# A gated linear recurrence followed by a SoLU feed-forward block: shorter weight conversion, first loads by batch, z turned from contiguous columns, and a new written sequence

## The chip, the cores and the metric

The kernel runs on one core of one Trainium2 chip. A core has five engines with a queue each, which run side by side and wait for one another through semaphores: TensorE (PE in the profile; PEld is its loading of weights), VectorE (DVE), ScalarE (ACT), GpSimd (POOL) and SyncE (SP), whose queue issues nearly all transfers here. The metric is the device time of one execution in microseconds. The kernel before took 447.55 us, the median of five runs (446.79 to 448.53).

## The reference

Inputs are q, k, v, a_re and a_im with 4 batches, 8 heads, 768 steps and 48 channels, all float32; the weights w_in (384 x 1024) and w_out (1024 x 384), which are given in float64, and g_ln (1024) in float32. The first block is a recurrence with a complex gate whose magnitude is held at 0.999 or below; only the real part is read out:

```python
scale = np.minimum(mag, 0.999) / (mag + 1e-06)
a_re_n, a_im_n = (a_re * scale, a_im * scale)
for t in range(S):
    new_re = ar * S_re - ai * S_im
    new_im = ar * S_im + ai * S_re
    kv = np.einsum('bhd,bhe->bhde', k[:, :, t], v[:, :, t])
    S_re, S_im = (new_re + kv, new_im)
    y[:, :, t] = np.einsum('bhd,bhde->bhe', q[:, :, t], S_re)
```

The heads of a step are put side by side (8 x 48 = 384 columns), which gives x with 3072 rows. The second block works row by row:

```python
h = x @ w_in
sm = softmax(h)                  # over the 1024 columns
solu = h * sm
ln = (solu - mean(solu)) / np.sqrt(var(solu) + 1e-06) * g_ln
out = ln @ w_out
```

## The kernel before, in words

The 768 steps are cut into 6 stretches of 128, and a stretch of one batch is a chunk; there are 24 chunks, numbered c = 4 * stretch + batch. Two chunks of one stretch form a group g; there are 12 groups. Within a chunk the recurrence becomes products: the running product of the gates is computed as the running sum of their logarithms and angles, q and k are multiplied by the grown and decayed factors and by cosine and sine, and then a masked product of scores, a product with v, and a carried state for each batch give the 128 rows of y.

The function `whole` does this. It defines each piece of work as a named step and then writes the steps out by hand in one sequence: the strings `START`, `EVEN`, `ODD` and `END`. The engines take their instructions in just this sequence, so it fixes the order in each queue. `START` runs once. Then a loop over n = 2 to 19 runs `EVEN` for even and `ODD` for odd n; in these, a number behind the colon is added to n, and g1, g2, g3 stand for group n // 2 plus 1, 2, 3. `END` runs once. SP's queue is in this sequence too: a transfer that has to wait holds up all transfers behind it.

The steps that the following speaks of:

- `load_ar`, `load_ai`, `load_q`, `load_k`, `load_v`, `load_vr` bring a group's inputs (L650, L660). ar and ai have 2 buffers, q, k and v have 3.
- `fetch:i`, `raised:i`, `convert:i` turn piece i of the weights from float64 to float32 with integer operations (L681; L688 and L690 on ACT; L696, L698 and L700 on DVE). There are 6 pieces of w_in with 512 columns and 8 of w_out with 384. The raw pieces have 6 buffers. `again` and `inspect` fetch and look at them a second time later. `mean`, `meansum` and `centre` (L714 to L724) fold g_ln and the mean over the 1024 rows into w_out.
- The gate chain of a group: `clamp`, `inverse` (ACT: Ln, Exp), `ratio`, `tangent`, `square`, `secant`, `size`, `eps`, `lnm`, then on PE `total` (tile f_L, L789), then `grow` and `decay` (ACT), `last` (a transfer of the last row), `ks` and `qs`; and with another table of functions on ACT (`trig`) `angle`, `on`, `phase` (PE, L843), `nearest`, `part`, `cos`, `sin`, and back with `exp`. In group 0 the first steps run in halves a and b, one for each chunk.
- `k2`, `q2` (L902) write k and q twice, times cosine and sine, into f_kq. For chunks 0 and 1, PE turns them (`kt`, `qt`) and ACT copies them (`kT`, `qT`). For the others `kqb` (L911) turns 32 x 32 blocks on DVE and `kqt0` (L916) moves the blocks with four DMAs into f_kqT.
- `score0`, `score1` (L958), `mask0` (L962), `values` (L990), `carry` (L998), `add` (L1007 to L1010) for the recurrence of a chunk.
- `turned_x` (L1024), `up0`, `up1` (L1030), `exp0` (L1035), `solu0` (L1039), `centred` (L1071), `spread` (L1074), `norm`, `down0`, `down1` (L1093), `scale` (L1097), `store` (L1102) for the feed-forward part. Between `solu0` and `down`, z must be turned. In chunks 0, 1, 2 and 23 (the list SHORT) PE does it (`zt`, `zT`); in the others `blocks` (L1058) turns 32 x 32 blocks on DVE and `away` (L1063) moves them with four DMAs into f_zT, from which `down` takes weights of 32 columns.

In `blocks`, column c * 128 + 4 * f + s of z goes to block s: the source is read with a step of four elements. So partition p of f_zT belongs to row c * 128 + p of w_out. PSUM holds h once (f_h), so `up` of the next chunk waits for `exp0` and `solu0` of the one before.

A second function, `general`, computes the same for any input and runs only if a check of the values at the end asks for it; the change doesn't touch it.

Of the kernel before, what the change touches and what calls it, by code (L numbers as in the profile page):

```python
# [11 lines left out]
FP = mybir.dt.float32  # L12
# [3 lines left out]
AF = mybir.ActivationFunctionType  # L16
# [3 lines left out]
P = 128  # L20
# [495 lines left out]
load_ar:0 load_ai:0 clampb:0 fetch:5 fetch:13 fetch:9 clampa:0 inverseb:0 ratiob:0 inversea:0 fetch:0 raised:5  # L516
tangentb:0 ratioa:0 squareb:0 raised:13 load_q:0 tangenta:0 secantb:0 sizeb:0 load_k:0 fetch:2 squarea:0
load_ar:1 fetch:11 raised:9 load_ai:1 secanta:0 convert:13 epsb:0 sizea:0 epsa:0 lnmb:0 lnma:0 fourthb:0
fourtha:0 total1:0 decay1:0 convert:5 convert:9 grow1:0 ks1:0 total0:0 grow0:0 decay0:0 trig:0 angleb:0 ks0:0
anglea:0 phase1:0 qs1:0 qs0:0 raised:0 phase0:0 nearest1:0 nearest0:0 raised:2 convert:0 part1:0 part0:0 cosb:0  # L520
load_vr:0 cosa:0 last:0 fetch:1 convert:2 sinb:0 clamp:1 sina:0 k2:0 q2:0 kt0:0 exp:0 qt0:0 inverse:1 load_v:0
k2:1 kT0:0 q2:1 qT0:0 ratio:1 raised:1 tangent:1 kt1:0 ends:0 convert:1 fetch:4 fetch:3 qt1:0 kT1:0 carry:1
fetch:6 raised:11 fetch:7 qT1:0 gain:0 turn_ends:0 kt0:1 tot:0 square:1 score0:0 convert:11 add:1 raised:4
score1:0 secant:1 kT0:1 onward:0 mask0:0 qt0:1 raised:3 fetch:12 fetch:8 raised:7 qT0:1 values:0 turned_x:0
kt1:1 fourth:1 qt1:1 kT1:1 up0:0 size:1 eps:1 convert:4 convert:3 qT1:1 up1:0 raised:12 convert:7 lnm:1 raised:6
raised:8 total1:1 convert:12 exp0:0 load_vr:1 total0:1 grow1:1 score0:1 decay1:1 convert:6 decay0:1 grow0:1
load_q:1 trig:1 load_k:1 convert:8 solu0:0 angle:1 carry:0 load_ar:2 fetch:10 score1:1 qs0:1 raised:10 phase1:1
phase0:1 nearest1:1 qs1:1 mask0:1 add:0 convert:10 nearest0:1 part1:1 mean:0 load_ai:2 part0:1 mean:2 ks0:1
clamp:2 mean:1 centred:0 mean:6 load_v:1 ks1:1 cos:1 mean:4 sin:1 last:1 k2:2 mean:3 mean:7 mean:5 values:1
zt0:0 meansum:0 load_k:2 load_vr:2 zt1:0 turned_x:1 q2:2 zT0:0 load_ai:3 centre:6 up0:1 exp:1 inverse:2 kqb:2  # L530
ratio:2 centre:5 kqt0:2 tangent:2 centre:0 centre:4 centre:3 up1:1 centre:2 spread:0 score0:2 centre:7 score1:2
exp0:1 square:2 secant:2 centre:1 size:2 mask0:2 eps:2 zT1:0 ends:1 down0:0 load_q:3 turn_ends:1 values:2 lnm:2
tot:1 total0:2 turned_x:2 total1:2 down1:0 load_q:2 fourth:2 k2:3 q2:3 decay1:2 grow0:2 decay0:2 solu0:1 norm:0
zt1:1 kqb:3 grow1:2 trig:2 up0:2 load_ar:3 angle:2 centred:1 zt0:1 scale:0 carry:2 qs1:2 again:1 last:2 ks1:2
onward:1 on:2 kqt0:3 zT1:1 phase0:2 store:0 zT0:1 phase1:2 spread:1 nearest1:2 score1:3 ks0:2 score0:3
nearest0:2 clamp:3 qs0:2 part1:2 part0:2 load_v:2 onward:2
"""
EVEN = """
add:0 cos:g1 mask0:1 up1:0 sin:g1 exp:g1 load_ai:g3 ends:g1 values:1 exp0:0 k2:2 q2:2 inverse:g2 norm:-1
down0:-1 kqb:2 solu0:0 ratio:g2 load_k:g2 down1:-1 turned_x:1 zt0:0 blocks:0 tangent:g2 zt1:0 again:-2 scale:-1  # L540
zT1:0 carry:1 k2:3 q2:3 inspect:-3 centred:0 spread:0 up0:1 kqt0:2 zT0:0 square:g2 secant:g2 size:g2 away:0
up1:1 kqb:3 eps:g2 lnm:g2 exp0:1 store:-2 score1:2 load_v:g2 add:1 score0:2 onward:g1 mask0:2 down0:0 solu0:1
total0:g2 store:-1 inspect:-2 total1:g2 fourth:g2 down1:0 norm:0 grow0:g2 decay0:g2 kqt0:3 blocks:1 turn_ends:g1
decay1:g2 grow1:g2 values:2 tot:g1 trig:g2
"""
ODD = """
angle:g2 scale:-1 qs0:g2 again:-2 turned_x:1 score1:2 on:g2 ks0:g2 load_ar:g3 score0:2 load_vr:g2 centred:0
ks1:g2 spread:0 phase0:g2 qs1:g2 phase1:g2 nearest0:g2 last:g2 nearest1:g2 clamp:g3 load_q:g3 away:0 part0:g2
part1:g2 carry:1 up0:1
"""  # L550
END = """
up1:20 mask0:21 cos:11 norm:19 store:18 sin:11 down0:19 exp:11 exp0:20 k2:22 q2:22 values:21 down1:19 kqb:22
solu0:20 k2:23 q2:23 turned_x:21 up0:21 centred:20 kqt0:22 score1:22 blocks:20 away:20 up1:21 spread:20 scale:19
kqb:23 score0:22 kqt0:23 down0:20 down1:20 mask0:22 norm:20 values:22 exp0:21 score0:23 solu0:21 blocks:21
score1:23 turned_x:22 up0:22 scale:20 mask0:23 store:20 away:21 up1:22 exp0:22 solu0:22 values:23 blocks:22
centred:22 turned_x:23 centred:21 down0:21 up0:23 spread:21 ends:11 spread:22 down1:21 norm:21 away:22 up1:23
norm:22 store:19 scale:21 down0:22 exp0:23 solu0:23 down1:22 zt0:23 scale:22 centred:23 store:21 zT0:23 zt1:23
spread:23 down0:23 zT1:23 norm:23 down1:23 scale:23 store:22 store:23
# [11 lines left out]
def whole(ctx, tc, flag, q, k, v, a_re, a_im, moe_w_in, moe_w_out, moe_g_ln, out):  # L570
# [40 lines left out]
    unit, quarter, small, mhalf, magic, mmagic = (bias[:, i:i + 1] for i in range(6))  # L611
# [32 lines left out]
    def load_steps(g):  # L644
        ti, b0 = g * GB // B, g * GB % B

        def load(nm, src, pl):
            def f():
                t = T[nm, g] = pl.tile([P, GB, DM], FP, tag=nm, name=f"f_{nm}")
                nc.sync.dma_start(out=t.rearrange("p b (h d) -> p (b h) d", d=D),  # L650
                                  in_=src[b0:b0 + GB, :, ti * P:(ti + 1) * P, :].rearrange("b h t d -> t (b h) d"))
            return f

        def reverse():

            vr = T["vr", g] = odds[g % 3]
            odd = v[b0:b0 + GB].rearrange("b h t d -> (b h) t d")[1::2]
            for r in range(0, P, 32):
                t0 = ti * P + P - 32 - r
                nc.sync.dma_start(out=vr[r:r + 32].rearrange("p b x w -> p (b x) w")[:, :, 16:],  # L660
                                  in_=odd[:, t0:t0 + 32, :].rearrange("h t d -> t h d"))

        return dict(load_ar=load("ar", a_re, ld), load_ai=load("ai", a_im, ld), load_q=load("q", q, ldv),
                    load_k=load("k", k, ldv), load_v=load("v", v, ldv), load_vr=reverse)

    def weight_steps():
# [11 lines left out]
        def fetch(i):  # L678
            w, wide, c, f0, n = pieces[i % len(pieces)]
            raw = rawp.tile([P, NW, 2], I32, tag="raw", name="f_raw")[:, 0:n]  # L680
            nc.sync.dma_start(out=raw.rearrange("p n u -> p (n u)"), in_=wide[:, c, 2 * f0:2 * (f0 + n)])  # L681
            T["raw", i] = raw

        def raised(i):
# [4 lines left out]
                                 scale=2.0 ** -29, bias=magic)  # L689
            nc.scalar.activation(out=y, in_=y.bitcast(FP), func=AF.Identity, bias=mmagic)  # L690

        def convert(i):
# [5 lines left out]
            nc.vector.scalar_tensor_tensor(out=x, in0=hi, scalar=-2 ** 30, in1=x, op0=OP.bitwise_and,  # L698
                                           op1=OP.bitwise_or)
            nc.vector.tensor_tensor(out=x, in0=x, in1=T["bits", i], op=OP.add)  # L700

# [317 lines left out]
    def ffn_steps(n):  # L1019
# [12 lines left out]

        def exp():
# [201 lines left out]
```

## Time and profile before

| | |
|---|---|
| median of 5 runs | 447.55 us (446.79 to 448.53) |
| the profiled execution, in all | 445.85 us |
| its span in the profile | 444.1 us |
| mean granted TensorE clock | 0.973 |
| HBM read and written | 38.87 and 4.72 MB |
| DMA issues into f_kqT | 88, 192 KB each, 3.4 us to landing (median) |
| DMA issues into f_zT | 80, 128 KB each, 2.9 us to landing (median) |
| table loads on ACT | 25 of 1283 ns |

Times in the profile are counted from the start of the span. The span leaves out a little on both sides of the program, so the profiled execution took 1.75 us more than it, and the median of the runs lies 1.70 us above that execution. A row of the page's groups gives the line, the engine, the operation, the tiles with their shapes, the count, then the busy time in us and the mean of one instruction in ns, and behind the second bar the time that the engine stood idle just before these instructions, and what ended most of it. Busy times of PE are modelled: its products overlap.

### The profile page before, as it was taken

What the parts mean: (1) busy time and instruction counts of PE and PEld (TensorE: products, weight loads), DVE (VectorE), ACT (ScalarE), POOL (GpSimd) and SP (SyncE); (2) the same over time, 40 slices, a digit from 0 to 9 for tenths busy, and PEclk for the clock granted to TensorE, in tenths of its full rate; (3) what the DMA queues carried; (4) which work ended last, traced back from release to release, by engine and by line L of the source; (5) the groups of instructions that cost most, each with busy time, mean ns of one, the idle gap of its engine ahead of it and who ended that gap; (6) DMA issues with size and microseconds to landing.
All of it is one profiled execution on the core that took longest, in us unless ns stands there. A gap on an engine that the chain in (4) does not pass through costs nothing.

```text
span 444.1 us, 13426 instructions
## 1 busy us (share of the span) xinstructions
PE 398.7 (90%) x5726; PEld 218.8 (49%) x5726; DVE 371.3 (84%) x516; ACT 282.7 (64%) x453; POOL 68.5 (15%) x141
## 2 busy tenths in 40 slices
PE   0238966989999999999999999999999999999992
PEld 0116643555755555645654554654655646545441
DVE  5689999878999999899999899899998998764310
ACT  3999996685776666656856756756757756620330
POOL 3000002103022041022121111120130130120210
PEclk9985898999999999999999999999999999999998
DMA  8984947486697797797798788878868666172210
GB/s 237 242 213 143 218 87 163 100 184 164 144 204 174 174 221 183 182 219 176 174 220 199 173 183 207 177 185 213 164 157 180 127 161 158 38 176 72 66 37 27
DMA packets 167716, 72.40 MB, mean 163 GB/s; under 512 B 142176, under 2 KB 155488, under 8 KB 167648
## 3 DMA queue, kind: packets, MB, share of 16 engines
q1 hardware_dynamic: 167504, 71.14, 69.6%
q8 instruction: 47, 0.77, 0.7%
q10 hardware_dynamic: 144, 0.33, 0.2%
q14 instruction: 21, 0.17, 0.1%
HBM read 38.87 MB, written 4.72 MB: 98 GB/s over the span
## 4 chain that ended last, share of the span: by engine, by line
PE 82%; DMA 5%; ACT 4%; DVE 4%; SPq 2%; issue 1%; POOL 0%; DVEq 0%; ACTq 0%
PE f_o L1093 29%; PE f_h L1030 26%; PE f_y L990 9%; PE f_score L958 6%; PE f_L L789 4%; PE f_phase L843 4%; PE f_d L998 3%; DMA f_kqT<-f_kb 2%; DMA f_raw<-in_moe_w_in_dram 2%; DVE f_kq L902 1%; DMA f_raw<-in_moe_w_out_dram 1%; SPq L916 1%; ACT f_bits L690 1%; ACT f_bits L688 1%; SPq L650 1%
## 5 line engine op out<-in xcount | busy, mean ns | idle before, releaser
L1093 PE MATMUL f_o<-f_w_out,f_zT 128*32 128x384 f32 (+1 forms) x1344 | 131.8, 487 | 0.2 <-ACT f_zT L1052 0.2
L1030 PE MATMUL f_h<-f_w_in,f_xT 128*128 128x512 f32 x288 | 130.4, 600 | 0.0
L1093 PEld LDWEIGHTS f_o<-f_w_out,f_zT 128*32 128x32 f32 (+1 forms) x1344 | 52.5, 114 | 64.6 <-issue 56.8
L1030 PEld LDWEIGHTS f_h<-f_w_in,f_xT 128*128 128x128 f32 x288 | 52.6, 190 | 59.4 <-issue 57.2
L911 DVE STREAM_TRANSPOSE f_kb<-f_kq 128x1536 f32<-128x1536 f32 x22 | 52.1, 2370 | 1.5 <-DMA f_kqT<-f_kb 1.2
L1071 POOL TENSOR_SCALAR f_less<-f_sum 128x1 f32<-128x1 f32 x24 | 13.1, 549 | 202.7 <-DVE f_z L1039 202.7
L1097 ACT ACTIVATE f_ot<-f_o,f_rs 128x384 f32<-128x384 f32 x24 | 13.8, 573 | 48.1 <-issue 36.6
L1058 DVE STREAM_TRANSPOSE f_zb<-f_z 128x1024 f32<-128x1024 f32 x20 | 43.4, 2170 | 0.1
L1039 DVE SCALAR_TENSOR_TENSOR f_z<-f_h,f_z 128x1024 f32<-128x1024 f32 x24 | 28.9, 1206 | 14.4 <-ACT f_z L1035 14.4
L1035 ACT ACTIVATE f_z<-f_h 128x1024 f32<-128x1024 f32 x24 | 24.4, 1017 | 24.5 <-PE f_h L1030 24.5
L958 PEld LDWEIGHTS f_score<-f_kqT 96*32 96x32 f32 x1536 | 31.7, 114 | 16.1 <-issue 8.4
L958 PE MATMUL f_score<-f_kqT 96*32 96x96 f32 (+3 forms) x1536 | 34.5, 242 | 5.2 <-DMA f_kqT<-f_kb 5.0
L990 PE MATMUL f_y<-f_att,f_v 128*16 128x128 f32 (+1 forms) x384 | 37.4, 280 | 0.6 <-DVE f_att L962 0.6
L990 PE MATMUL f_y<-f_att,f_vr 128*32 128x128 f32 x384 | 37.2, 281 | 0.0
L789 PE MATMUL f_L<-f_lr,f_mats 128*128 128x384 f32 x48 | 19.9, 539 | 18.2 <-DVE f_lr L784 18.2
L962 DVE TENSOR_TENSOR f_att<-f_score,f_mats 128x1024 f32<-128x1024 f32 x24 | 29.1, 1215 | 7.0 <-PE f_score L958 7.0
L990 PE MATMUL f_y<-f_kqT,f_state 96*32 96x128 f32 (+1 forms) x640 | 32.3, 272 | 0.0
L1074 ACT ACTIVATE f_z<-f_z,f_less 128x1024 f32<-128x1024 f32 x24 | 27.5, 1145 | 3.7 <-DVE f_zb L1058 2.6
L1080 POOL TENSOR_SCALAR f_s<-f_s,f_sum 128x1 f32<-128x1 f32 x24 | 15.1, 630 | 75.6 <-ACT f_z L1074 74.9
L793 ACT ACTIVATE f_ai<-f_L 128x384 f32<-128x384 f32 x24 | 12.0, 499 | 22.6 <-PE f_L L789 22.6
L1024 ACT COPY f_xT<-f_y 128x384 f32<-128x384 f32 x24 | 11.3, 473 | 23.6 <-PE f_y L990 23.6
L990 PEld LDWEIGHTS f_y<-f_att,f_v 128*16 128x16 f32 (+1 forms) x384 | 20.9, 105 | 10.0 <-issue 8.5
(102 smaller groups left out, 641.4 us busy)
## 6 DMA issues: line engine op xcount, KB each, us to landing
f_kqT<-f_kb SPq DMA_DIRECT2D x88, 192.0 KB, 3.4
f_zT<-f_zb SPq DMA_DIRECT2D x80, 128.0 KB, 2.9
f_raw<-in_moe_w_in_dram SPq DMA_DIRECT2D x12, 512.0 KB, 6.2
f_raw<-in_moe_w_out_dram SPq DMA_DIRECT2D x16, 384.0 KB, 5.3
f_ar<-in_a_re_dram SPq DMA_DIRECT2D x12, 384.0 KB, 5.5
f_ai<-in_a_im_dram SPq DMA_DIRECT2D x12, 384.0 KB, 4.1
f_q<-in_q_dram SPq DMA_DIRECT2D x12, 384.0 KB, 4.6
f_k<-in_k_dram SPq DMA_DIRECT2D x12, 384.0 KB, 5.1
```

Source lines behind the costliest of these rows:

```text
L789: nc.tensor.matmul(out=ps, lhsT=tri, rhs=st["lr"][:, i * DM:(i + 1) * DM], start=True, stop=True)
L843: nc.tensor.matmul(out=ps, lhsT=turns, rhs=st["x0"][:, i * DM:(i + 1) * DM], start=True, stop=True)
L911: nc.vector.transpose(out=t, in_=T["kq", c].rearrange("p n h (f j) -> p j (n h) f", j=3))
L958: nc.tensor.matmul(out=scores[r0:r0 + 32, x, r:], lhsT=QK[:, r // 32, x], rhs=QK[:, r // 32:, H + x], start=True, stop=True)
L962: nc.vector.tensor_tensor(out=st["att"].rearrange("p (i u) t -> p i u t", u=2), in0=scores.rearrange("p (i u) t -> p i u t", u=2), in1=mat ...
L990: nc.tensor.matmul(**product)
L1030: nc.tensor.matmul(out=st["h"][:, half * 512:(half + 1) * 512], lhsT=st["xT"][:, c * P:(c + 1) * P], rhs=w_in[:, c, half * 512:(half + 1) ...
L1035: nc.scalar.activation(out=st["z"], in_=st["h"], func=AF.Exp, accum_out=sums[:, n:n + 1])
L1039: nc.vector.scalar_tensor_tensor(out=st["z"], in0=st["h"], scalar=1.0, in1=st["z"], op0=OP.mult, op1=OP.mult, accum_out=st["sum"][:, 0:1])
L1058: nc.vector.transpose(out=st["zb"], in_=st["z"].rearrange("p (c f s) -> p s c f", s=4, f=32))
L1074: nc.scalar.activation(out=st["z"], in_=st["z"], func=AF.Square, bias=st["less"], accum_out=st["sum"][:, 1:2])
L1093: nc.tensor.matmul(out=st["o"][rows], lhsT=zT, rhs=w_out[:, c], start=(c == 0), stop=(c == KF - 1))
```

## The change

It has four parts.

1. `raised` has one ACT operation in place of two; `convert` has the same three DVE operations with other constants and the addition in the middle.
2. For group 0, `load_ar` and `load_ai` are split into two transfers each, one for each chunk: `load_ara`, `load_aia`, `load_arb`, `load_aib`.
3. `blocks` reads 32 neighbouring columns for a block. So that the result fits, w_out's rows are fetched in another sequence (partition 4 * f + s gets row c * 128 + 32 * s + f), g_ln is fetched by four DMAs in the same sequence, and in the four chunks that PE turns, `exp0` writes z in that sequence and `solu0` works in four parts. Their four sums are added by two more POOL operations in `centred`.
4. `START`, `EVEN`, `ODD` and `END` are new. Two more table loads on ACT (`trig:0`, `exp:30`) stand at the start.

The core of the diff; of the four strings the whole of the new `EVEN` and `ODD` and the parts of the new `START` that matter here:

```diff
 START = """
+trig:0 load_ara:0 load_aia:0 exp:30 load_arb:0 clampa:0 inversea:0 ratioa:0 tangenta:0 load_aib:0 squarea:0
+secanta:0 clampb:0 fetch:9 sizea:0 inverseb:0 epsa:0 ratiob:0 fetch:5 tangentb:0 lnma:0 fetch:4 raised:5
+squareb:0 fetch:0 raised:9 convert:5 secantb:0 fetch:2 fourtha:0 sizeb:0 fourthb:0 epsb:0 total0:0 convert:9
+raised:0 decay0:0 lnmb:0 fetch:13 total1:0 load_q:0 grow0:0 load_k:0 raised:4 raised:13 grow1:0 convert:0
+raised:2 decay1:0 trig:30 convert:4 convert:13 convert:2 angleb:0 anglea:0 last:0 phase1:0 fetch:11 load_ar:1
...
+part1:0 sina:0 qs1:0 convert:11 cosb:0 load_vr:0 fetch:7 k2:0 kt0:0 sinb:0 q2:0 clamp:1 exp:0 ends:0 kT0:0 qt0:0
+k2:1 turn_ends:0 qT0:0 kt1:0 tot:0 inverse:1 q2:1 qt1:0 kT1:0 qT1:0 qt0:1 fetch:8 carry:1 ratio:1 kt0:1 score0:0
+add:1 kT0:1 tangent:1 qT0:1 fetch:12 score1:0 mask0:0 raised:1 square:1 qt1:1 raised:3 convert:1 fetch:10 kt1:1
...
 EVEN = """
+score0:2 tangent:g2 k2:3 square:g2 q2:3 secant:g2 fourth:g2 size:g2 kqb:3 load_k:g2 down0:0 eps:g2 spread:0
+lnm:g2 add:1 score1:2 load_ar:g3 exp0:1 total0:g2 total1:g2 grow1:g2 down1:0 decay0:g2 mask0:2 decay1:g2
+grow0:g2 kqt0:3 solu0:1 trig:g2 load_ai:g3 ends:g1 turn_ends:g1 ks1:g2 values:2 score1:3 angle:g2 score0:3
+ks0:g2 onward:g1 blocks:1 again:-5 on:g2 qs1:g2 phase0:g2 turned_x:2 last:g2 norm:0 tot:g1 away:1 carry:2
+nearest0:g2 qs0:g2 phase1:g2 mask0:3 nearest1:g2 add:2 scale:0 load_v:g2 part0:g2 part1:g2 cos:g2 inspect:-4
+clamp:g3 up0:2
 ODD = """
+centred:0 again:-3 inspect:-6 sin:g2 values:2 load_q:g3 k2:3 q2:3 exp:g2 kqb:3 store:-2 up1:1 down0:0 inverse:g3
+exp0:1 store:-1 turned_x:2 carry:2 solu0:1 centred:1 down1:0 spread:0 blocks:1 ratio:g3 up0:2 up1:2 norm:0
+scale:0 kqt0:3 load_vr:g2 away:1
...
@@ fetch
-            nc.sync.dma_start(out=raw.rearrange("p n u -> p (n u)"), in_=wide[:, c, 2 * f0:2 * (f0 + n)])
+            rows = wide[:, c, 2 * f0:2 * (f0 + n)]
+            if w is w_out:
+                rows = rows.rearrange("(s f) x -> f s x", s=4)
+            nc.sync.dma_start(out=raw.rearrange("p n u -> p (n u)"), in_=rows)
@@ raised
             nc.scalar.activation(out=y.bitcast(FP), in_=T["raw", i][:, :, 0].bitcast(U32), func=AF.Identity,
-                                 scale=2.0 ** -29, bias=magic)
-            nc.scalar.activation(out=y, in_=y.bitcast(FP), func=AF.Identity, bias=mmagic)
+                                 scale=-2.0 ** -51, bias=mtwo)
@@ convert
-            nc.vector.scalar_tensor_tensor(out=x, in0=hi, scalar=-2 ** 30, in1=x, op0=OP.bitwise_and,
-                                           op1=OP.bitwise_or)
             nc.vector.tensor_tensor(out=x, in0=x, in1=T["bits", i], op=OP.add)
+            nc.vector.scalar_tensor_tensor(out=x, in0=hi, scalar=2 ** 30 - 1, in1=x, op0=OP.bitwise_or,
+                                           op1=OP.bitwise_and)
@@ exp
+            if n in SHORT:
+                z, h = z.rearrange("p (c f s) -> p c s f", s=4, f=32), h.rearrange("p (c s f) -> p c s f", s=4, f=32)
+            nc.scalar.activation(out=z, in_=h, func=AF.Exp, accum_out=sums[:, n:n + 1])
@@ solu
+            parts = [(st["h"], st["z"])]
+            if n in SHORT:
+                parts = [(st["h"].rearrange("p (c s f) -> p s c f", s=4, f=32)[:, s],
+                          st["z"].rearrange("p (c f s) -> p s c f", s=4, f=32)[:, s]) for s in range(4)]
+            for i, (h, z) in enumerate(parts):
+                nc.vector.scalar_tensor_tensor(out=z, in0=h, scalar=1.0, in1=z, op0=OP.mult, op1=OP.mult,
+                                               accum_out=st["sum"][:, 2 + i:3 + i])
@@ blocks
-            nc.vector.transpose(out=st["zb"], in_=st["z"].rearrange("p (c f s) -> p s c f", s=4, f=32))
+            nc.vector.transpose(out=st["zb"], in_=st["z"].rearrange("p (c s f) -> p s c f", s=4, f=32))
@@ centred
+            if n in SHORT:
+                half, total = st["sum"][:, 2:4], st["sum"][:, 0:1]
+                nc.gpsimd.tensor_tensor(out=half, in0=half, in1=st["sum"][:, 4:6], op=OP.add)
+                nc.gpsimd.tensor_tensor(out=total, in0=st["sum"][:, 2:3], in1=st["sum"][:, 3:4], op=OP.add)
@@ gain
+        for s in range(4):
+            nc.sync.dma_start(out=g_ln[s:P:4], in_=moe_g_ln.rearrange("(c s f) -> f s c", s=4, f=32)[:, s])
```

## The prediction

> **What bounds the kernel now.** I read the page first (engine shares, the 40 slices), then the busy times in three stretches, then the chain that ended last, then the groups by shape, and last the queue of each engine in order of time.
>
> ```profile
> span 444.1 us, 13426 instructions
> PE 398.7 (90%) x5726; PEld 218.8 (49%) x5726; DVE 371.3 (84%) x516; ACT 282.7 (64%) x453; POOL 68.5 (15%) x141
> PEclk9985898999999999999999999999999999999998
> ...
> 0.00:92.88 92.88, 55.79 (x570) 34.03 (x571) 76.86 (x143) 72.97 (x123) 9.52 (x24) 0.89 0.74 177
> 92.88:436.20 343.32, 342.85 (x5156) 184.76 (x5156) 294.12 (x373) 209.16 (x329) 58.95 (x117) 1.00 0.71 162
> 436.20:444.10 7.90, 0.08 (x2) 0.00 (x0) 0.29 (x2) 0.58 (x1) 0.00 (x0) 0.77 0.12 37
> ```
>
> The columns of the three stretches are PE, PEld, DVE, ACT, POOL, granted clock, DMA share, GB/s. TensorE (PE) is busy for 342.85 of 343.32 us in the middle stretch: there only its own work sets the time. Ahead of 92.88 us it idles 37 us, while VectorE (DVE) and ScalarE (ACT) are at 83% and 79%. So the change can gain ahead of 92.88 us, or by giving TensorE less to do.
>
> ```profile
> 66.68 2.25 DVE f_kb L911
> 70.98 4.02 DMA f_kqT<-f_kb
> ...
> 88.19 4.45 DMA f_kqT<-f_kb
> 92.88 1.28 PE f_score L958 x34
> ...
> 136.85 5.35 PE f_h L1030 x12
> 142.20 1.24 PE f_score L958 x34
> ...
> 152.30 1.10 PE f_score L958 x34
> ...
> 378.88 5.15 PE f_h L1030 x12
> ...
> 391.09 2.77 PE f_h L1030 x6
> 393.86 0.68 PE f_score L958 x17
> 394.54 2.79 PE f_h L1030 x6
> 397.34 0.68 PE f_score L958 x17
> ```
>
> The chain (start, length) says who hands over: DVE turns k and q of chunk 3 (`kqb:3`, 83.91 to 86.2 us), a transfer brings them, and the scores of chunk 3 start at 92.88, after which only TensorE is in the chain. The last rows show a price of order: `up` and `score` halved and alternated take 2.77+0.68+2.79+0.68 = 6.92 us, undivided 5.35+1.24 = 6.59. One more stretch of full 128x128 products (up, L, phase, turns) between products in 32-wide pieces costs 0.33: about 0.19 on entering (up is 5.15 behind phase, 5.35 else), 0.14 on leaving (scores 1.24 behind up, 1.10 else).
>
> ```profile
> L911 DVE STREAM_TRANSPOSE f_kb<-f_kq 128x1536 f32<-128x1536 f32 x22 | 52.1, 2370 | 1.5 <-DMA f_kqT<-f_kb 1.2
> L1058 DVE STREAM_TRANSPOSE f_zb<-f_z 128x1024 f32<-128x1024 f32 x20 | 43.4, 2170 | 0.1
> ```
>
> These are groups by shape (busy us, mean ns, idle before). The turn of z takes 2.12 ns an element with a source step of four elements, that of k and q 1.54 with three; a plain pass over 1024 elements (L1039) takes 1.21 us.
>
> [...] the 25 loads here have 1283. [...] here the granted clock is 0.54 at 30 to 40 us and 0.61 at 40 to 50.
>
> **The change part by part.**
>
> *One ScalarE operation a piece.* Removed: L690, 8 x 615 + 6 x 722 ns = 9.2 us of ACT, all ahead of 62 us. Some 3.3 us of it is in the chain (0.72+0.61+0.61+0.72+0.61). VectorE still does three operations a piece. Their reordering I cost at nothing, bounds -0.1 to +0.1 us a piece (before, a dependent successor starts 0.13 us after the end).
>
> *First loads by batch.* Four DMAs for two. The first ar landed for DVE at 5.46 us and ai at 7.20; with half the bytes I take 4.2 and 5.0. ACT has two more table loads at the start (2.57 us): 0.72 + 3 x 1.28 = 4.6 us, just before the first clamp is done (4.8), so they are hidden; if the load comes sooner, they cost up to 0.5. But six weight pieces now lie ahead of q and k in SP's queue, and `last:0`, which waits for the decays (about 21.9), stands ahead of the loads for group 1.
>
> *z from contiguous columns.* 20 turns; if the step was the whole cost, each falls from 2.17 to about 1.2 us (bounds 1.1 and 2.17): 1.9 us of DVE per loop pass. TensorE covers this: worth nothing on the path. In chunks 0, 1, 2 and 23 the exponential writes, and four DVE operations of 256 elements read and write, with a step of 16 bytes. One operation of 1.24 us becomes four: at least 4 x 0.36 = 1.45, at most, with the doubled element cost, 4 x 0.6 = 2.4. Two of these chunks lie ahead of `kqb:3`: +0.4 to +2.4 us. In chunk 23 they are covered by `down:22` (5.3 us on PE); the two small POOL additions (0.3 to 0.5 each) by `down` as well. w_out's rows come in another sequence, with the same 3 KB each; g_ln by four issues for one, +1.9 us of SP, needed only at `mean:0`.
>
> *The new sequence, start.* By hand, with the durations above: lnm of half a at 13, squares and convert:5 next, the second half's at 17.5, decays done 21.9 (before 22.1), tables 23.3, phases done 27 (half clock), part, cos, sin; first `k2:0` at 30.6 (before 31.62). Then the array at half clock sets the pace: copies of kT0, qT0, `inverse:1` (1.8) between, kT1, qT1 at 37.0, then on PE a turn (1.05), carry (1.5), a turn (1.05) and the scores (2.36): `mask0:0` at 42.6 (before 42.93). The gain at the first load is mostly given back there. From `mask0:0` to the end of `kqb:3` DVE took 43.3 us before (42.93 to 86.2) and was busy for 40.3 of them; after, the same instructions lie between these two (7 weight pieces, all 8 centres, both k and q turns), summing to 0.1 more, and the split solu, for which I take +0.9 (the lower half of its bounds: DVE waits 1.8 us for PE in this stretch, 0.67 at a mask and 1.12 at tot, and the longer solu takes up some of that). So `kqb:3` ends at 42.6 + 43.4 + 0.9 = 86.9. Issue and landing take 6.5 (before 86.2 to 92.88 = 6.7): scores of chunk 3 at 93.4.
>
> *The new sequence, from there.* Before: 343.4 us of PE remain (436.3 - 92.88). After: the second half of up:2 now comes first, -2.9. The loop pass before: 5.35+1.24+2.60+1.49+2.72+0.15+1.90+1.10+1.51+0.81+5.35+1.90+5.16+0.67 = 31.95 (the chain's period is 31.96). After, with phase split by carry, up by values, score by down: .68+2.58+.55+1.49+2.72+.15+1.90+1.10+.83+.81+.83+2.58+1.90+2.77+2.72+.67+2.58+5.37 = 32.23, one full stretch more. 9 passes: +2.5. Outside the loop some three more stretches and a tot: +1.1. Remaining 344.1. The tail (last product to the end: scale, store, flag) is unchanged: 7.8.
>
> Sum: 93.4 + 344.1 + 7.8 = 445.3 us span, against 444.1. The profiled execution had 445.85 in all (1.75 beside its span), and the median of the runs stands 1.70 above it: 445.3 + 3.45 = 448.8.
>
> **Rivals.**
>
> *The start gains more than the loop loses (faster).* Place: DVE between `k2:0` and `k2:2`. If PE's slow turns don't hold it (ACT has 9.2 us less in its queue), DVE needs from 30.6 on only its own 28.2 + 1.4 (dependencies in seven pieces) + 0.5 = `k2:2` at 60.7 against 64.3. Then kqb:3 ends at 83.8, and the span is 83.8+6.5+344.1+7.8 = 442.2, the median 445.6. It decides once `kqb:3` ends before 85.0; with turns at full clock a further 2 us go. For it: DVE idled 14 of the 86.2 us before `kqb:3` ended, 10.4 of them ahead of the first k2. Against: carry, tot and the mask need PE, whose granted clock was 0.50 from 31.6 to 42.9 us and 0.53 still at 46 to 48.
>
> *A late zT in every pass.* In the odd half SP issues kqT (2.6), then four vr loads, then zT (2.6). kqb ends 21.5 us into the pass, so zT is issued to 29.4 and lands 2.9 later, at 32.3; `down0` wants it at 32.9. But four vr took 5.57 us at 180 us, and one zT set 4.37. A wait of 0.4 to 1 us in nine passes gives 452 to 458.
>
> *The turn of z is not cheaper.* Then DVE has 1.9 us a pass more; it enters the even half 3.8 us ahead of PE rather than 5.7, and `score1`, turned in the same pass, has 0.9 us to spare rather than 2.8: still hidden, 449 to 451.
>
> *The loop was VectorE's.* DVE is busy 30.72 of 31.96 us a pass. Were it the bound, the cheaper turn would give 9 x 1.9 = 17 us, 431. Against: PE's pieces in the tail, where DVE is idle, are as long as in the loop (5.37, 5.18, 1.11); I give it almost nothing.
>
> **How the numbers follow.** My forecast, within 446.5 to 451: 0.40. Start gains: 0.35. zT late: 0.20. The rest 0.05. Under 0.2% (0.9 us), about what a measurement of this kernel can tell from no change, lies 0.13, nearly all from my case. Faster 0.37: the first rival and a little of my case; slower 0.50: the rest of my case, the late zT, the dear turn. Range 442 to 456: down to the first rival with a warm array, up through most of the second.
>
> **What would show it.** Right: L690's successor gone, 14 operations on ACT; first k2 near 30.6; `kqb:3` ending near 87; scores of chunk 3 near 93.4; a pass of 32.2 us, with PE idle under 1 us in all; the z turn near 1.2 us. Wrong: `kqb:3` before 85 (first rival), a PE wait for a transfer into f_zT or f_kqT in the loop (second), a z turn of 2.17 us, split solu pieces of 0.6 us. If PE's alternation costs nothing in the loop, the pass stays at 31.96 and 2.5 us come off.

## The result and the profile after

The changed kernel takes 445.63 us (median of 28 runs, 443.94 to 448.90), the kernel before beside it 447.55 (49 runs). The ratio is 0.9962, with a 95% interval of 0.9950 to 0.9974: faster by 0.38%, or 1.7 us. The forecast was 448.8, slower. The range (442 to 456) held the time; the sign was wrong.

The page of the kernel after, its span, engines and granted clock by slice:

```profile
span 442.2 us, 13453 instructions
PE 402.8 (91%) x5726; PEld 218.9 (50%) x5726; DVE 361.0 (82%) x540; ACT 280.4 (63%) x441; POOL 63.7 (14%) x149
PEclk9999988999999999999999999999999999999998
```

TensorE (PE) is busy 4.1 us longer than before (398.7), and yet the span is 1.9 us shorter: PE idles 39.4 us instead of 45.4. VectorE (DVE) has lost 10.3 us of work, which the span doesn't show.

The busy times of the kernel after, cut where the prediction cut them (columns as there: PE, PEld, DVE, ACT, POOL, granted clock, DMA share, GB/s):

```profile
0.00:91.14 91.14, 58.77 (x579) 33.14 (x583) 79.71 (x155) 70.55 (x114) 9.97 (x24) 0.96 0.75 175
91.14:435.38 344.24, 343.97 (x5152) 185.77 (x5151) 281.00 (x384) 209.24 (x327) 53.75 (x125) 1.00 0.71 163
435.38:442.20 6.82, 0.08 (x2) 0.00 (x0) 0.29 (x2) 0.58 (x1) 0.00 (x0) 0.71 0.13 43
```

The three terms of the sum are there one by one, in one execution of each kernel. The scores of chunk 3 start at 91.14 (before 92.88, forecast 93.4). From there PE has 344.24 us (before 343.32, forecast 344.1). What lies behind its last product takes 6.82 (before 7.90, forecast 7.8). So the start gave 1.74, the middle took 0.92, the end gave 1.08.

The chain that ended last, kernel after (start, length, what):

```profile
69.63 3.69 DVE f_w_out L734 x7
73.45 4.29 PE f_o L1116 x8
...
91.14 0.68 PE f_score L968 x17
...
150.07 0.87 PE f_phase L853 x2
150.94 0.81 PE f_d L1008 x48
151.75 0.84 PE f_phase L853 x2
```

Before, the chain went from `kqb:3` over a transfer to the scores at 92.88. Now it goes over the centring of w_out to `down0:0` at 73.45, and PE works without a gap from there; the scores of chunk 3 find their transfer landed (at 90.70, 0.4 us before they start). The rows at 150 show `carry` (f_d) between the two phases, which makes the additional stretch of full products that the prediction priced. `up` starts at 133.52, 165.81 and 198.10: a pass of 32.29 us (before 31.96, forecast 32.23).

The groups by shape, kernel after (busy us, mean ns, idle before):

```profile
L1076 DVE STREAM_TRANSPOSE f_zb<-f_z 128x1024 f32<-128x1024 f32 x20 | 24.8, 1242 | 0.4
L1058 DVE SCALAR_TENSOR_TENSOR f_z<-f_h,f_z 128x256 f32<-128x256 f32 x16 | 9.2, 639 | 9.7 <-ACT f_z L1049 9.7
```

The turn of z takes 1242 ns instead of 2170. With neighbouring columns it runs at 1.21 ns an element, the pace of a plain pass in this kernel (1219 ns for 1024 elements). The quarter solu takes 639 ns for 256 elements, 2.5 ns an element.

### The profile page after: what moved, and what is told of

Same layout as the page of the kernel before. It is cut to its first block, busy times and chain, and to the rows that moved or that the text cites. A ratio compares the mean times of both kernels' runs of the same rounds, so it can differ in the third digit from the quotient of the medians.

```text
span 442.2 us, 13453 instructions
## 1 busy us (share of the span) xinstructions
PE 402.8 (91%) x5726; PEld 218.9 (50%) x5726; DVE 361.0 (82%) x540; ACT 280.4 (63%) x441; POOL 63.7 (14%) x149
## 4 chain that ended last, share of the span: by engine, by line
PE 83%; DVE 8%; ACT 4%; issue 2%; DMA 1%; POOL 0%; DVEq 0%; POOLq 0%
PE f_o L1116 28%; PE f_h L1040 27%; PE f_y L1000 9%; PE f_score L968 6%; PE f_phase L853 5%; PE f_L L799 4%; PE f_d L1008 3%; DVE f_w_out L734 1%; DMA f_ar<-in_a_re_dram 1%; ACT f_bits L699 1%; DVE f_kq L912 1%; ACT L898 1%; DVE f_kb L921 1%; PE f_zt L1068 1%; PE f_turned L933 0%
## 5 line engine op out<-in xcount | busy, mean ns | idle before, releaser
L1116 PE MATMUL f_o<-f_w_out,f_zT 128*32 128x384 f32 (+1 forms) x1344 | 135.5, 489 | 0.5 <-DVE f_w_out L734 0.3
L1116 PEld LDWEIGHTS f_o<-f_w_out,f_zT 128*32 128x32 f32 (+1 forms) x1344 | 54.9, 114 | 65.8 <-issue 50.5
L1058 DVE SCALAR_TENSOR_TENSOR f_z<-f_h,f_z 128x1024 f32<-128x1024 f32 (+1 forms) x36 | 33.6, 961 | 22.9 <-ACT f_z L1049 22.9
L1049 ACT ACTIVATE f_z<-f_h 128x1024 f32<-128x1024 f32 x24 | 28.6, 1190 | 15.9 <-PE f_h L1040 15.9
L1000 PE MATMUL f_y<-f_att,f_v 128*32 128x128 f32 (+1 forms) x384 | 37.0, 275 | 0.4 <-DVE f_att L972 0.4
L968 PE MATMUL f_score<-f_kqT 96*32 96x32 f32 (+3 forms) x1536 | 35.3, 237 | 2.0 <-DMA f_kqT<-f_kb 2.0
L1094 POOL TENSOR_SCALAR f_less<-f_sum 128x1 f32<-128x1 f32 x24 | 5.1, 214 | 190.0 <-DVE f_z L1058 162.7
L856 ACT ACTIVATE f_f<-f_phase,f_bias 128x384 f32<-128x384 f32 x24 | 13.9, 581 | 27.1 <-PE f_phase L853 26.9
L853 PE MATMUL f_phase<-f_x,f_mats 128*128 128x384 f32 x48 | 22.9, 578 | 6.7 <-ACT f_x L839 6.7
L912 DVE TENSOR_TENSOR f_kq<-f_cs,f_k 128x768 f32<-128x768 f32 x24 | 22.8, 951 | 4.1 <-ACT f_cs L870 3.4
```

Of the source, the lines that this page charges most:

```text
L853: nc.tensor.matmul(out=ps, lhsT=turns, rhs=st["x0"][:, i * DM:(i + 1) * DM], start=True, stop=True)
L912: nc.vector.tensor_tensor(out=t, in0=T["cs", g][:, i * H:(i + 1) * H], in1=heads(T[nm, g][:, i]).unsqueeze(2).to_broadcast([P, H, 2, D]), ...
L968: nc.tensor.matmul(out=scores[r0:r0 + 32, x, r:], lhsT=QK[:, r // 32, x], rhs=QK[:, r // 32:, H + x], start=True, stop=True)
L1000: nc.tensor.matmul(**product)
L1049: nc.scalar.activation(out=z, in_=h, func=AF.Exp, accum_out=sums[:, n:n + 1])
L1058: nc.vector.scalar_tensor_tensor(out=z, in0=h, scalar=1.0, in1=z, op0=OP.mult, op1=OP.mult, accum_out=st["sum"][:, 2 + i:3 + i])
```

## The experiments

Each kernel was timed beside runs of the kernel before on the same chip, so two of them are compared by their ratios; 0.001 of the ratio is 0.45 us. Medians in us.

| kernel | what it is | median | ratio to before, 95% interval |
|---|---|---|---|
| after | the change | 445.63 | 0.9962 (0.9950 to 0.9974) |
| two_ops | after, two ScalarE operations a piece | 452.29 | 1.0105 (1.0078 to 1.0132) |
| whole_loads | after, first loads whole | 446.97 | 0.9992 (0.9974 to 1.0010) |
| strided_z | after, z as before | 445.01 | 0.9947 (0.9932 to 0.9961) |
| b_one_op | before, one ScalarE operation a piece | 445.12 | 0.9948 (0.9928 to 0.9968) |
| b_one_op_loads | the same, first loads by batch | 445.67 | 0.9957 (0.9938 to 0.9977) |
| old_order | all of the change but the sequence | 448.23 | 1.0014 (1.0000 to 1.0029) |
| m1_carry | after, carry ahead of the phases | 442.89 | 0.9896 (0.9874 to 0.9918) |
| m2_up | and up whole | 442.04 | 0.9879 (0.9855 to 0.9902) |
| b_one_op_carry | b_one_op, carry ahead of the phases | 443.77 | 0.9914 (0.9883 to 0.9946) |
| warm | after, six more products on PE | 445.46 | 0.9952 (0.9936 to 0.9969) |
| warm3 | after, three more | 444.09 | 0.9925 (0.9898 to 0.9953) |
| short23 | after, chunks 0 to 2 turned on VectorE | 454.50 | 1.0144 (1.0115 to 1.0174) |
| best | m2_up + short23 + warm3 | 452.52 | 1.0100 (1.0070 to 1.0130) |
| m1_warm3 | m1_carry + warm3 | 442.15 | 0.9891 (0.9862 to 0.9920) |
| m2_warm3 | m2_up + warm3 | 440.73 | 0.9860 (0.9832 to 0.9888) |

### Which part made the start faster

**Two operations again.**

```diff
-                                 scale=-2.0 ** -51, bias=mtwo)
+                                 scale=2.0 ** -29, bias=magic)
+            nc.scalar.activation(out=y, in_=y.bitcast(FP), func=AF.Identity, bias=mmagic)
```

> The kernel after with the two ScalarE operations a weight piece put back (and VectorE's three in their old sequence); all else as after. Theory A (the start gains because ScalarE's queue is shorter): four pieces stand in the chain between 16 and 20.8 us, so each added operation of 0.61 to 0.72 us moves the first table load, the phases and the first k2 (29.25 us) by 2 to 2.6 us, and the median rises by 1.5 to 2.6 us, to 447.1 to 448.2. Rival B (the earlier first loads and the sequence make the gain, ScalarE's queue has room): first k2 moves by under 0.7 us, the median by under 0.5, to at most 446.1.

Measured: 452.29, 6.4 us above after by the ratios, more than twice what theory A asked. (VectorE's three operations went back to their old order with it.) ScalarE's (ACT) queue in time, two_ops, from the first half's L on:

```profile
18.22 0.72 ACT L701 ACTIVATE f_bits<-f_bits,f_bias 128x512 int32<-128x512 f32 x1
...
23.34 0.72 ACT L701 ACTIVATE f_bits<-f_bits,f_bias 128x512 int32<-128x512 f32 x1
23.97 0.47 ACT L807 ACTIVATE f_ar<-f_L 128x384 f32<-128x384 f32 x1
24.46 1.28 ACT L899 ACT_TABLE_LOAD   x1
```

The decays (L804, L807) stand behind the weight pieces in one queue; the table load that follows them starts at 24.46 instead of 20.84. That moves the first k2 from 29.25 to 32.97 and mask0:0 from 40.05 to 43.57. Between mask0:0 and mask0:1 a further 3.6 us come (66.23 for 59.06), where the pieces of 40 to 52 us stand in ACT's queue. So the new sequence doesn't merely gain from the removal, it can't do without it.

**First loads whole.**

```diff
-trig:0 load_ara:0 load_aia:0 exp:30 load_arb:0 clampa:0 inversea:0 ratioa:0 tangenta:0 load_aib:0 squarea:0
+trig:0 load_ar:0 load_ai:0 exp:30 clampa:0 inversea:0 ratioa:0 tangenta:0 squarea:0
```

> The kernel after with the first a_re and a_im loaded whole, as before (two DMAs for four); all else as after. Theory B (the earlier first loads make the gain): the first half's clamp starts at 5.5 instead of 4.5 us and its a_im comes at 7.2 instead of 5.4, so L of the first half comes 1.8 us later (15.0 for 13.2), the first k2 1 to 1.8 us later, and the median rises by 0.8 to 1.8, to 446.4 to 447.4. Rival A (ScalarE's queue): the first half has slack to the second, which sets the decays; first k2 moves by under 0.5, the median by under 0.4.

Measured: 446.97, by the ratios 1.3 us above after. The first k2 comes at 30.75 (+1.50), mask0:0 at 41.39 (+1.34), the k and q turn of chunk 3 at 83.69 (+1.53). A delay at the first load arrives at the end nearly whole: theory B holds too, beside A. Nothing of it was "given back".

**Everything but the sequence; and the operations alone in the old sequence.**

> The kernel after with the four written sequences of before (the first loads still by batch, each pair adjacent; no early table loads): everything in the change but the new sequence. If the operations alone make the start faster (one ScalarE operation, earlier loads), the start keeps most of the 1.7 us by which scores of chunk 3 came earlier, and the loop is back at 31.96 us a pass, so 442 to 444. If the new sequence makes the start, the start is as before or, with the split solu of chunks 0 to 2, later: 446.5 to 449.

> The kernel before with one ScalarE operation a weight piece, nothing else. Theory A (ScalarE's queue): in the chain of before three of the removed operations (0.72+0.61+0.61) stand ahead of the decays and two more later, so the first k2 comes 1.3 to 1.9 us earlier and the median falls by 1 to 3 us, to 444.5 to 446.5. Rival: the old sequence waits for the raw weight pieces (10.7 us in the chain) and for TensorE's slow turns, so the median falls by under 0.9 us, 446.7 to 447.5.

> The kernel before with one ScalarE operation a weight piece and the first a_re and a_im loaded by batch, the second batch's (whose clamp comes first in the old sequence) ahead. It parts the 3.1 us by which old_order (448.2) stands above b_one_op (445.1) into loads and z's layout. If z's layout costs them (split solu, strided exponential, g_ln by four issues): 444.1 to 445.3 here. If the loads by batch do (two more issues on SP's queue, transfers later behind them): 447 to 448.

Measured: 448.23, 445.12 and 445.67. In the old sequence one operation a piece gives 2.3 us (theory A's range). The earlier loads give nothing there: the first clamp starts at 4.74 instead of 5.52, but L, which the old sequence does for both halves together, stays at 15.98 (15.92) and the first k2 at 29.05 (28.99). With z's new layout as well, old_order stands 2.5 us higher (1.0014 against 0.9957); it also loads the halves of a_re ahead of those of a_im, another order than b_one_op_loads has, but its first k2 comes no later for that (28.50). Taking the parts in this order, the whole change is -2.3 (ScalarE) + 0.4 (loads, within the uncertainty of none) + 2.5 (z) - 2.3 (sequence).

The parts depend on each other. With z's old layout the new sequence gives only 0.4 us, within the uncertainty of none (strided_z, below, at 0.9947 against 0.9957 for b_one_op_loads, give or take 1.1 us). And one operation a piece alone (b_one_op, 0.9948) is as fast as the whole change (0.9962), within the uncertainty.

Where the 2.3 us come from in the old sequence, in the kernel before (start, length; f_L is `total`, L902 is `k2`, L962 is `mask0`):

```profile
11.49 0.72 ACT L690 ACTIVATE f_bits<-f_bits,f_bias 128x512 int32<-128x512 f32 x1
13.18 0.61 ACT L690 ACTIVATE f_bits<-f_bits,f_bias 128x384 int32<-128x384 f32 x1
15.27 0.61 ACT L690 ACTIVATE f_bits<-f_bits,f_bias 128x384 int32<-128x384 f32 x1
18.19 2.93 PE L789 MATMUL f_L<-f_lr,f_mats 128*128 128x384 f32 x4 [18.19 <-DVE f_lr L784]
31.62 0.96 DVE L902 TENSOR_TENSOR f_kq<-f_cs,f_k 128x768 f32<-128x768 f32 x1 [0.27 <-ACT f_cs L860]
42.93 1.21 DVE L962 TENSOR_TENSOR f_att<-f_score,f_mats 128x1024 f32<-128x1024 f32 x1
```

and in b_one_op:

```profile
15.92 2.92 PE L788 MATMUL f_L<-f_lr,f_mats 128*128 128x384 f32 x4 [15.92 <-DVE f_lr L783]
28.99 0.95 DVE L901 TENSOR_TENSOR f_kq<-f_cs,f_k 128x768 f32<-128x768 f32 x1
40.28 1.21 DVE L961 TENSOR_TENSOR f_att<-f_score,f_mats 128x1024 f32<-128x1024 f32 x1
```

Three of the removed operations stand among the steps of the first gate chain in ACT's queue, ahead of L. Without them L starts 2.27 us sooner, the first k2 2.63 and mask0:0 2.65. Between k2:0 and mask0:0 nothing is gained: 11.31 us in before, 11.29 in b_one_op, and the same to 0.03 us in the three other kernels with the old sequence. VectorE (DVE) is busy for 10.76 and 10.74 us of this stretch and shows no wait in it. So VectorE's own queue sets mask0:0 in the old sequence, and TensorE's pace doesn't: the 64 scores take 2.36 us in before and 1.33 in b_one_op, where they are done 3.3 us ahead of the mask.

**z as before.**

```diff
-            nc.vector.transpose(out=st["zb"], in_=st["z"].rearrange("p (c s f) -> p s c f", s=4, f=32))
+            nc.vector.transpose(out=st["zb"], in_=st["z"].rearrange("p (c f s) -> p s c f", s=4, f=32))
```

(with w_out's rows, g_ln, exponential, solu and sum of before)

> The kernel after with z laid out as before: the turn of z reads with a step of four elements (2.17 us for 1.24), w_out's rows and g_ln are loaded in their own sequence, and exponential and solu of chunks 0, 1, 2 and 23 are whole again. Theory (TensorE sets the loop, VectorE the start): the dearer turn costs nothing, and the start gains what the split solu (four of 0.64 and four accumulator reads for one of 1.22, in two chunks ahead of kqb:3) and the strided exponential cost, 2.5 to 3.2 us: 442.4 to 443.1. Rival (the new loop needs the cheaper turn): VectorE has 0.9 us more a chunk, TensorE waits in the loop, and the median is above 446.

Measured: 445.01, and by the ratios 0.7 us below after, the intervals overlapping. The dearer turn (18.6 us of DVE over 20 turns) costs nothing that shows, as theory said. The start's gain is half seen: the k and q turn of chunk 3 starts at 79.64 instead of 82.16, 2.5 us sooner, but `down0:0` only at 72.60 instead of 73.45. So in the new sequence the turn of chunk 3 is no longer alone in setting the end, and the 2.5 to 3.2 us of the theory didn't come. The rival isn't wholly excluded: in the one profiled execution the shortest pass takes 32.28 us, as in after, but the mean of seven is 32.73 (after 32.39), with halts of PE like those described further down.

### The slow array

> The kernel after with six further products (128x384, result not read) on TensorE between the first phases and the first turn of k, where it idles for 4.6 us: the array goes on working. If TensorE's slow turns and carry (1.96 us for eight turns, 1.50 for the first carry) still hold the start, they are done at full speed, mask0:0 starts 1 to 2 us sooner than 40.05, and the median falls by up to 1.6 us, to 444.0. If VectorE's own work sets the start, mask0:0 comes sooner but kqb:3 doesn't, and the median stays within 0.4 of 445.6.

> The kernel after with three further products (result not read) on TensorE between the first phases and the first turn of k, so that they end at about 30.2 us, when the first turn starts. With six, the first turn came 3 us late and mask0:0 0.5 us late, so that the fast array gave back 2.5 us. If the slow array holds the start, mask0:0 comes at 38 to 39 instead of 40.05 us and the median falls by 0.6 to 1.5, to 444.1 to 445.0. If VectorE's own work holds it, the median stays within 0.4 of 445.6.

```diff
+    def warm():
+        ps = ps_t.tile([P, DM], FP, tag="t", padded_shape=[P, 512], name="f_warm")
+        for i in range(3):
+            nc.tensor.matmul(out=ps, lhsT=ident, rhs=mats[:, 0:3].rearrange("p n t -> p (n t)"), start=True, stop=True)
...
-part1:0 sina:0 qs1:0
+part1:0 warm:0 sina:0 qs1:0
```

Measured: 445.46 with six, 444.09 with three. PE's queue in warm3:

```profile
30.92 1.09 PE L933 MATMUL f_turned<-f_mats,f_kq 128*96 128x128 f32 x8
...
35.40 0.88 PE L1008 MATMUL f_d<-f_v,f_kq 128*32 128x48 f32 x48
...
36.79 1.33 PE L968 MATMUL f_score<-f_kqT 96*32 96x128 f32 x64
```

Eight turns take 1.09 us (after 1.96), the first carry 0.88 (1.50). In after, VectorE waits for the carry and for the scores:

```profile
37.62 0.55 DVE L1020 TENSOR_TENSOR f_state<-f_d,f_tot 96x384 f32<-96x384 f32 x1 [1.19 <-PE f_d L1008]
...
40.05 1.22 DVE L972 TENSOR_TENSOR f_att<-f_score,f_mats 128x1024 f32<-128x1024 f32 x1 [0.41 <-PE f_score L968]
```

In warm3 it shows neither wait. mask0:0 starts at 38.41 instead of 40.05, `down0:0` at 71.71 instead of 73.45, and by the ratios the time falls by 1.7 us, give or take 1.3. With six, the first turn starts 3 us late, at 33.24, but mask0:0 only 0.5: eight turns take 1.04 us there, and 2.5 us came back. Why the turns behind the added products are faster isn't shown: the granted clock from 30 to 40 us is 1.00 in after as in warm3.

The gain isn't the same in each execution. The same three products stand in three later kernels: in m1_warm3, m2_warm3 and best the eight turns took 1.33, 1.63 and 1.70 us, and mask0:0 came at 38.43, 39.14 and 40.36. Nor is the pace without them a constant: the 64 scores took 2.36 us in before and 1.51 in after, but 1.33 in b_one_op and in m1_carry (below), which has the start of after; neither has an added product. So the slow array did hold the start of the new sequence, as the prediction said, by the 1.6 us of these two waits; in the old sequence it held nothing at mask0:0.

### The price of a stretch, and what takes it back

```diff
-ks0:g2 onward:g1 blocks:1 again:-5 on:g2 qs1:g2 phase0:g2 turned_x:2 last:g2 norm:0 tot:g1 away:1 carry:2
+ks0:g2 onward:g1 blocks:1 again:-5 on:g2 qs1:g2 turned_x:2 last:g2 norm:0 tot:g1 away:1 carry:2 phase0:g2
```

for m1_carry, and for m2_up also

```diff
-centred:0 again:-3 inspect:-6 sin:g2 values:2 load_q:g3 k2:3 q2:3 exp:g2 kqb:3 store:-2 up1:1 down0:0 inverse:g3
+centred:0 again:-3 inspect:-6 sin:g2 up1:1 values:2 load_q:g3 k2:3 q2:3 exp:g2 kqb:3 store:-2 down0:0 inverse:g3
```

> The kernel after with carry moved in the even half from between phase0 and phase1 to ahead of phase0, so that phase0, phase1 and the first half of up are one stretch of full 128x128 products: one stretch less a pass. If a stretch costs 0.33 us, as the prediction priced it, a pass falls from 32.29 to 31.96 us, and the median by 9 x 0.33 = 3.0 to 442.6. If TensorE's pieces are only recorded differently, or the new place makes carry wait for the copy of x, the median stays at 445.6 or rises.

> As the one before, and the second half of up moved ahead of values in the odd half, so that phase0, phase1 and both halves of up are one stretch: two stretches less a pass than after. At 0.33 us each a pass falls to 31.63 us and the median by 6 us, to 439.6. If the price isn't causal: 445.6. If values, 2.6 us later, makes the copy of x and the next up late, there is a new wait for f_xT and the median lies between 442.6 and 448.

> The kernel before with one ScalarE operation a weight piece, and carry moved in the odd half from between phase1 and up0 to ahead of phase0, so that phase and up are one stretch. If a stretch costs 0.33 us: a pass of 31.62 us, and the median 9 to 10 x 0.33 us below the 445.1 of the same kernel with the old place of carry: 442.0. If the price of a stretch isn't causal: 445.1.

Measured: by the ratios -3.0 us for one stretch (forecast -3.0), -3.7 for two (-6), and -1.5 for one in the old sequence (-3). The chain of m1_carry shows the merged stretch, in a pass of 31.94 us (265.60 to 297.54):

```profile
282.15 0.68 PE f_d L1008 x48
282.83 1.49 PE f_phase L853 x4
284.32 2.58 PE f_h L1040 x6
```

carry and the phases take 0.68 + 1.49 instead of 0.87 + 0.81 + 0.84, 0.35 less. The shortest passes carry the price throughout: 31.95 us in before and 31.60 in b_one_op_carry, 32.28 in after, 31.93 in m1_carry, 12.89 + 18.72 = 31.61 in m2_up. In the times it came in full only for the first stretch; m2_up's second one gave 0.7 us, and the 1.5 of b_one_op_carry has an uncertainty of 1.7. Where the rest went is seen in the passes: over seven passes of m2_up (122.51 to 346.97) the mean is 32.07, after's over seven (133.52 to 360.28) is 32.39, and over seven of b_one_op_carry it is 32.12 against 32.10 in b_one_op, each in one execution. PE's queue in m2_up, one such pass:

```profile
143.84 0.39 PE L968 MATMUL f_score<-f_kqT 96*32 96x128 f32 x6
144.00 0.49 PE L1116 MATMUL f_o<-f_w_out,f_zT 128*32 128x384 f32 x1
144.32 0.73 PE L968 MATMUL f_score<-f_kqT 96*32 96x32 f32 x26
```

`down` and the scores hang for some 0.4 us between two of their products; the profile shows no semaphore that is late. In m1_carry the same at 185.89, at the last scores ahead of carry:

```profile
185.89 0.22 PE L968 MATMUL f_score<-f_kqT 96*32 96x32 f32 x1 [0.66 <-issue]
```

"issue" means that the profile shows nothing that PE waited for. Most of these halts stand at the scores, where PE has 64 short products in 1.1 us (in b_one_op_carry two stand at carry), and they come in some passes of every kernel whose passes are given here (in before one pass takes 32.50 us for 31.96). That PE's instructions came late there, as the expectation of m2_warm3 has it, is my reading; no run shows it. Besides, TensorE, now earlier, waits 1.6 us at 109 us for the transfer of chunk 4's k and q in m1_carry and m2_up.

> The kernel after with carry ahead of the phases (-2.7 us measured alone) and the three further products (-1.5 measured alone). If start and loop add up: 441.4. If the earlier start only runs into the transfer of chunk 4's k and q (TensorE waited 1.6 us for it at 109 us in each of these), 442.9.

> As the one before with the second half of up ahead of values too (-3.6 us measured for both moves). If they add up: 440.5. If TensorE's waits for instructions at the scores take back what the cleaner order gives (clean passes took 31.6, their mean 32.1): 441.5 to 442.5.

Measured: 442.15 and 440.73. Start and loop add up for m2 (by the ratios 4.6 us below after, of 3.7 + 1.7), and hardly for m1 (3.2, of 3.0 + 1.7); the intervals are 2.6 us wide, so this part stays open. m2_warm3 is the fastest kernel of the study, 1.40% below before (0.9860, 0.9832 to 0.9888).

### The short chunks on VectorE

```diff
-    SHORT = [0, 1, 2, 23]
+    SHORT = [23]
-decay1:1 load_q:1 total0:1 grow1:1 grow0:1 convert:12 convert:6 decay0:1 score0:1 solu0:0 trig:1 angle:1
+decay1:1 load_q:1 total0:1 grow1:1 grow0:1 convert:12 convert:6 decay0:1 score0:1 solu0:0 blocks:0 away:0 trig:1 angle:1
```

(likewise for chunks 1 and 2)

> The kernel after with chunks 0, 1 and 2 treated like the chunks of the loop: whole exponential and solu, z turned on VectorE and sent by DMA (solu, then blocks, then away), no turn of z on TensorE; only chunk 23 keeps TensorE's. VectorE: 1.22 + 1.24 us a chunk for four pieces of 0.56 with 0.08 each = 2.5, no change; ScalarE loses 1.0 us an exponential and two copies a chunk; TensorE loses 3 x 0.87 us of turns. If the layout's price in these chunks is what keeps the new code from gaining more, the median falls by 1.5 to 3.5 us, to 442.1 to 444.1. Rival: zT by DMA lands too late for down in the start, TensorE waits there, and the median is 445.5 or more.

> The kernel after with three edits at once: carry ahead of the phases and the second half of up ahead of values, chunks 0 to 2 like those of the loop, and the three further products. If they add up: 445.6 - 3.6 (measured for the first two) - 1.5 to 3.5 - 0 to 1.5 = 437.0 to 440.5. If the loop then waits for instructions or transfers that TensorE used to give time for, it stays at 440.5 to 442.

Measured: 454.50 and 452.52; the rival's side, and by more than theory or rival reckoned. SP's waits in short23 from 40 to 130 us by cause (us in total, times, longest), one row:

```profile
SPq L1080 <- DVE f_zb L1075: 16.5, 3, 10.5
```

DVE's queue in short23:

```profile
94.07 0.95 DVE L756 TENSOR_SCALAR_CACHE_REDUCE f_ar<-f_ar 128x768 f32<-128x768 f32 x1 [6.07 <-DMA f_ar<-in_a_re_dram]
```

and PE's waits:

```profile
PE f_score L967 <- DMA f_kqT<-f_kb: 9.0, 2, 6.5
```

The transfers of `away` (L1080) wait in SP's queue for DVE's turn, once for 10.5 us (from 69.6 to 80.2), and every load behind them waits along: a_re of group 3 is issued at 87.6 instead of 77.6, and DVE stands 6.07 us for it. The transfer of chunk 3's k and q stands behind these loads too: their turn ends at 84.22, but it is issued at 89.84, and the scores wait 6.5 us for it, until 96.86 (after 91.14). `down` wasn't late, as the rival had it: PE shows no wait for a transfer into f_zT. By this trace the place of the transfer in the queue was the price, not its landing; no run puts it elsewhere.

## Why the prediction was wrong

**The step that failed: the hand-made timeline of the start**, "`mask0:0` at 42.6 (before 42.93)", with its reason, "the array at half clock sets the pace", and the conclusion, "The gain at the first load is mostly given back there". mask0:0 started at 40.05. Half of the 2.55 us lies ahead of k2:0 (29.25, forecast 30.6): L of the second half started at 17.52, as forecast (17.5), but the table load after the decays at 20.84, while I had the decays done at 21.9. The other half lies behind k2:0: 10.8 us to mask0:0 for the forecast 12.0, 0.85 of it in the 64 scores. (The terms of the timeline after 37.0 add up to 42.96, not to 42.6.)

The reason was misread from before. There the stretch from k2:0 to mask0:0 took 11.31 us because VectorE's own queue filled it; the slow array ran beside it and held nothing, as b_one_op shows. The new sequence takes work out of that stretch. Seven of the 14 weight pieces are converted on VectorE ahead of k2:0 (before five) and none between k2:0 and mask0:0 (before two). VectorE is busy there for 9.10 us (before 10.76), and ahead of k2:0 it idles 6.4 us (before 10.4). Only then does the array hold the stretch, by the 1.6 us of waits. This is read from the two traces; no run moves these pieces alone.

**From mask0:0 on the sum held.** To the end of `kqb:3` 44.44 us (forecast 44.3): VectorE had 2.0 us more work there than before (42.25 for 40.26), and 0.8 less idle time, so 1.2 of the 2.0 arrived, for a forecast of 1.0. From there to the scores 6.65 (6.5). In this second one chance helped: PE was itself busy until 91.14, and the transfer had landed. "kqb:3 decides" was right for before and no longer for after.

**The loop: right.** A pass of 32.29 (32.23), the rest of PE's work 344.24 (344.1); the price of 0.33 us a stretch is there in the shortest passes, and in the time of m1_carry.

**The end: 1 us too long, not seen.** From ACT's last eviction to the end of the span: 7.19 us in before, 6.20 in after, and 6.15 to 6.38 in the nine experiments on after with its turns of z on TensorE or its old z layout; 7.15 to 8.88 in the four with the old sequence, 9.18 and 8.77 in short23 and best. Each kernel was profiled in one execution: that nine lie within 0.23 us speaks for the program rather than the execution, but the five with the old ending differ by 1.7 among themselves. The cause is open; the prediction had "The tail ... is unchanged". It is 1.0 of the 3.1 us by which the span was missed (2.26 start, 0.98 end, -0.14 loop).

**ScalarE's operations:** 9.2 us removed, as forecast, and worth 2.3 us in the old sequence, 6.4 in the new. "Some 3.3 us of it is in the chain" was nearer than the timeline made of it. Of convert in its new order no cost is seen, but no run has it alone.

**First loads:** 4.52 and 5.43 us (forecast 4.2 and 5.0), worth 1.3 us (give or take 1.0) in the new sequence and nothing that shows in the old. The two table loads are hidden: the second ends at 4.58, and the first logarithm waits for DVE's clamp until 5.12.

**z's turn:** 1242 ns (forecast 1.2 us), and worth nothing on the path, as forecast (strided_z). **Split solu:** four of 0.64 us, which the prediction had named as a sign of being wrong; 2.17 and 2.33 us from start to end in chunks 0 and 1, inside the bounds of 1.45 to 2.4, but 0.9 and 1.1 more than one operation (1.22), where I took 0.9 for both together. **Not in the sum at all:** the strided exponential, 2.05 us for 1.00 (L1049 against L1035), and one on ACT in each of these chunks: the step of 16 bytes in its writes doubled the operation. The prediction had put a cost on this step for DVE alone. The layout as a whole shows a price of 2.5 us in the old sequence and 0.7, within the uncertainty, in the new; its parts weren't tried apart.

**The rivals.** The first came true: k2:2 at 61.60 (60.7), `kqb:3` ended at 84.5 (83.8, deciding below 85.0), span 442.2, median 445.63 (445.6). That the last two are met to the tenth is luck: `kqb:3` was 0.7 us later than the rival had it, and the end 1.0 shorter. Its mechanism came in part: from k2:0 to k2:2 VectorE needed 32.35 us, not the 30.1 of its own work, and k2:0 came 1.35 sooner. A late zT: PE shows no wait for f_zT by transfer in any pass of after; in short23 a zT did hold up SP's queue in the start, but the loads behind it came late, not `down`. The dearer turn: its turn didn't come, and strided_z, where it is as dear as before, took 445.0, though without the split solu. The loop wasn't VectorE's.

## What to carry to other kernels

An in-order queue is read by what stands behind each item, not by its busy share: ACT was 64% busy, and yet three operations of 0.6 to 0.7 us in its queue held the first gate chain, and with it everything behind it, by 2.3 us. Before a slow engine is put into a hand-made timeline, look whether anything waits for it. In before the engine behind the slow products had a full queue of its own, so their pace cost nothing; in after two pieces of work had left that queue, and the pace cost 1.6 us. In a reordering, count the switches between full and narrow products on PE. Each stretch costs 0.33 us a pass here, and taking one out of each pass was worth 3.0 us, more than the 1.7 of the whole change; the second gave only 0.7. And a part of a change can be as good as the whole: one ScalarE operation less, alone, was.

## What the runs showed of the hardware

- Three products without use, in PE's idle time, made the kernel 1.7 us faster (warm3, give or take 1.3). The eight turns behind them took 1.09 us there and 1.33 to 1.70 in three other kernels with the same products (after 1.96). The granted clock of the record doesn't tell it in time: after has 1.00 between 30 and 40 us, while its eight turns took 1.96 us there (1.08 later).
- An exponential that writes with a step of 16 bytes takes 2.05 us for 1024 columns, one that writes in sequence 1.00; a DVE product with such a step 639 ns for 256 columns, 1219 for 1024 without. A stream transpose with neighbouring columns takes 1242 ns, with a step of 16 bytes 2170.
- PE's halts, most of them at the scores, 0.2 to 1.4 us with nothing late that the profile shows, took back about half of what fewer switches gave a pass in m2_up, and all of it in the profiled execution of b_one_op_carry.
- The time behind the last eviction differed by up to 3 us between the profiled executions (6.15 to 9.18) of kernels that end in the same work.
